# Five of nine sign passes read from PSUM, routing's small steps and four subtractions moved to GpSimd, and a new set of order offsets

## The chip, the cores and the metric

The kernel runs on one core of one Trainium2 chip. The metric is the time of one execution on the device in microseconds (us), lower is better. Times given for a kernel are medians of several runs; the profile is of one more execution, whose own time is given beside its span.

The core's engines are named as the profile names them: PE is the matrix engine (PEld its weight loads), DVE the vector engine, ACT the scalar engine, POOL is GpSimd, and SP is the engine that here only starts transfers. Matrix products land in PSUM, all else lives in SBUF.

## The reference, cut to what matters

Attention with a top-32 mask over 8 x 8 heads of 576 rows of 64 numbers, and then a mixture of 8 experts in which every token that is not skipped takes one expert:

```python
scores = scale * q @ k.T                                  # 64 heads, 576 x 576
kth = np.partition(scores, -32, axis=-1)[..., -32:-31]
scores = np.where(scores >= kth, scores, -1e9)
attn = exp(scores - max) / (sum + 1e-9)
x = (attn @ v) -> 4608 tokens x 512
do_compute = x @ w_skip > 0
logits = x @ w_gate;  e_idx = argmax(logits, axis=1)
gate_w = softmax(logits)[e_idx]
out = x;  out[do_compute] += gate_w * (relu(x @ w1[e_idx]) @ w2[e_idx])
```

Every row of scores needs its 32nd largest value, so each row of 576 scores is searched, not only exponentiated.

## The kernel before, in words

**Attention, some 860 us.** Two heads make a pair; there are 32 pairs (`NP`), and nine row tiles of 128 rows (`NR`) in each, 288 in all. For one row tile the function `row` records these steps:

- PE computes 128 x 576 scores into one of three PSUM buffers of rows (`qk`, L652). The class `Hold` keeps the buffer until its readers have given it back.
- DVE finds the eight largest of each of seven chunks (`chunk`, L662), and then the 24 largest of those 56 (`cand`: L668 and L670 by turns, five steps, each of which needs the one before).
- ACT copies the scores from PSUM to SBUF (`take`, L704). After it the PSUM buffer is free: `take` is its only reader beside the chunk search.
- ACT takes the sign of each score against the 24th largest (`above_out`, L684), with the sum of the signs as a second output. It reads the SBUF copy, and its bias is one number per partition (a column of the tile `cl`).
- POOL multiplies copy and signs (`push_out`, L707), DVE fills nine more columns (`fill`, L716) and takes the eight largest of what is left (`window`, L728); the last of these is the threshold.
- ACT writes the penalty (`below_out`, L725): again from the SBUF copy, with one number per partition as bias.

When a pair's rows are done, nine "units" compute the transposed scores in the same three PSUM buffers (L867, L869), subtract the penalties (L874) and are read by one exponential on ACT (L899). Products with V, sums, and the gate's logits follow.

**Routing.** After the batches 0 to 3, after 4 to 6 and after 7 (`GROUPS`), the function `route` turns the gate's logits into lists of tokens: a chain of some 20 small steps of at most 128 x 160 elements, all on DVE, with one exponential and one copy on ACT and one product on PE between them (L410 to L450), and then per batch the lists (`lists`, L469 to L487), partly on POOL. The first two groups run during attention, the third at its end.

**Experts, some 300 us.** Weights are split in a high part (ACT, `part_hi`, L1109) and a low part (DVE, `part_lo`, L1112), tokens are gathered by index (POOL, L1139), and PE does three products for one. The first expert's weights are split while the last pair is still at work.

**What sets the order.** Nothing is issued in the order in which it is written. Each step is put in a plan (`pl.add`) with its engine, a duration, a due time and the steps it needs; `Plan.run` then picks, engine by engine, the next step by readiness and due time and emits it. The due times are a row's number plus offsets from the table `K` and, for each of the nine rows of a pair, from `FINE`. The order that comes out is fixed in the program: on the chip each engine works its list from the top, and a step that is not ready holds up what stands behind it.

Of the kernel before, what the change touches and what calls it, by code (L numbers as in the profile page):

```python
# [36 lines left out]
OUT = (0, 1, 2, 3, 4, 5, 6, 7, 8)  # L37
PD = ()
TD = ()
PP = ()  # L40
SA = 1
AD = ()


@with_exitstack
def tile_kernel(ctx, tc, q, k, v, w_skip, w_gate, w1, w2, out):
# [1545 lines left out]
```

## Time and profile before

| | |
|---|---|
| time, median of 3 runs | 1180.88 us (1179.74 to 1182.52) |
| the profiled execution's own time / its span | 1182.15 / 1180.3 us |
| PE busy, share of the span | 1117.7 us, 95% |
| DVE | 1000.2 us, 85% |
| ACT | 931.8 us, 79% |
| POOL | 752.6 us, 64% |
| granted PE clock over the span | 0.98 of full speed |

The span is the time from the first to the last instruction. A record's duration can overlap the one before it on its engine by some tenths of a us, so a group's count times its mean is more than the time it took. PE's busy time is modelled and says little. The busy time of the engines has to be read by stage: in attention PE, DVE and ACT are all busy for nearly the whole time, in the experts' stage PE alone is.

### The profile page before, as it was taken

What the parts mean: (1) busy time and instruction counts of PE and PEld (TensorE: products, weight loads), DVE (VectorE), ACT (ScalarE), POOL (GpSimd) and SP (SyncE); (2) the same over time, 40 slices, a digit from 0 to 9 for tenths busy, and PEclk for the clock granted to TensorE, in tenths of its full rate; (3) what the DMA queues carried; (4) which work ended last, traced back from release to release, by engine and by line L of the source; (5) the groups of instructions that cost most, each with busy time, mean ns of one, the idle gap of its engine ahead of it and who ended that gap; (6) DMA issues with size and microseconds to landing.
All of it is one profiled execution on the core that took longest, in us unless ns stands there. A gap on an engine that the chain in (4) does not pass through costs nothing. (4 is left out here: it accounts for less than half of the span.)

```text
span 1180.3 us, 37612 instructions
## 1 busy us (share of the span) xinstructions
PE 1117.7 (95%) x13012; PEld 947.0 (80%) x13012; DVE 1000.2 (85%) x5250; ACT 931.8 (79%) x1965; POOL 752.6 (64%) x997
## 2 busy tenths in 40 slices
PE   4899999999999999999999999999889999999996
PEld 3778888888888888788877878877778988888885
DVE  8999999999999999999999999999954756655531
ACT  5999999999999999999998999999862533333320
POOL 7778888777888877788875999777772112222210
PEclk8799999999999999999998999999999999999998
DMA  5545555644556554455544454443065654454300
GB/s 122 123 113 122 134 129 131 159 115 113 124 135 145 139 134 113 115 129 137 141 121 120 105 131 124 123 115 83 22 191 181 197 164 149 152 162 156 116 19 25
DMA packets 197404, 148.42 MB, mean 126 GB/s; under 512 B 100898, under 2 KB 162850, under 8 KB 197204
## 3 DMA queue, kind: packets, MB, share of 16 engines
q1 hardware_dynamic: 190340, 135.54, 44.8%
q0 software_dynamic: 3840, 9.47, 2.5%
q8 instruction: 105, 1.72, 0.6%
q10 hardware_dynamic: 3024, 0.90, 0.3%
q14 instruction: 95, 0.78, 0.2%
HBM read 68.31 MB, written 25.31 MB: 79 GB/s over the span
## 5 line engine op out<-in xcount | busy, mean ns | idle before, releaser
L707 POOL TENSOR_TENSOR xw<-xc,r 128x576 f32<-128x576 f32 x288 | 370.3, 1286 | 148.8 <-ACT r L684 143.4
L662 DVE MAX8 cand<-r 128x8 f32<-128x82 f32 (+1 forms) x2016 | 366.7, 234 | 3.0 <-PE r L652 2.9
L684 ACT ACTIVATE r<-xc,cl 128x576 bf16<-128x576 f32 x288 | 224.8, 780 | 16.3 <-DVE cl L668 15.3
L725 ACT ACTIVATE PEN<-xc,wn 128x576 bf16<-128x576 f32 x288 | 224.5, 780 | 3.7 <-DVE wn L728 3.6
L728 DVE MAX8 wn<-xw 128x8 f32<-128x585 f32 x288 | 217.2, 754 | 2.4 <-POOL xw L707 2.2
L867 PE MATMUL r<-QH,KK 128*128 128x256 f32 (+1 forms) x640 | 190.3, 324 | 10.1 <-ACT PT L899 4.5
L704 ACT ACTIVATE xc<-r 128x576 f32<-128x576 f32 x288 | 188.6, 655 | 9.5 <-DVE cand L662 3.9
L652 PE MATMUL r<-KK,QH 128*128 128x288 f32 x640 | 162.2, 344 | 14.0 <-ACT xc L704 6.6
L869 PE MATMUL r<-QL,KK 66*128 66x256 f32 (+1 forms) x640 | 174.5, 300 | 0.0
L668 DVE MAX8 cl<-cand 128x8 f32<-128x28 f32 (+2 forms) x864 | 166.7, 193 | 4.4
L899 ACT ACTIVATE PT<-r 128x576 f32<-128x576 f32 x256 | 166.9, 654 | 3.1 <-PE r L874 2.9
L1146 POOL DMA_INDIRECT out_dram<-ot,idx x24 | 24.5, 1022 | 213.8 <-DVE ot L1145 167.2
L1112 DVE TENSOR_TENSOR lo<-raw,hi 128x1024 fp32r<-128x1024 f32 x64 | 79.2, 1241 | 72.0 <-ACT hi L1109 71.1
L652 PE MATMUL r<-KK,QL 66*128 66x288 f32 x640 | 135.1, 302 | 0.0
L867 PEld LDWEIGHTS r<-QH,KK 128*128 128x128 f32 x640 | 119.0, 192 | 17.5 <-ACT PT L899 7.4
L874 PE MATMUL r<-nbi,PEN 128*128 128x128 bf16 (+1 forms) x1632 | 132.8, 217 | 0.0
L652 PEld LDWEIGHTS r<-KK,QH 128*128 128x128 f32 x640 | 98.2, 196 | 41.0 <-ACT PT L899 12.2
L1109 ACT ACTIVATE hi<-raw 128x1024 fp32r<-128x1024 f32 x64 | 67.2, 1055 | 71.6 <-PE py L1241 71.4
L869 PEld LDWEIGHTS r<-QL,KK 66*128 66x128 f32 x640 | 119.9, 193 | 0.3 <-issue 0.2
L652 PEld LDWEIGHTS r<-KK,QL 66*128 66x128 f32 x640 | 103.9, 194 | 0.3 <-issue 0.3
L1221 ACT ACTIVATE hh<-ph 128x352 fp32r<-128x352 f32 (+2 forms) x72 | 31.1, 433 | 92.5 <-PE ph L1218 89.4
L670 DVE MATCH_REPLACE8 cand<-cl,cand 128x28 f32<-128x28 f32 x576 | 103.3, 179 | 0.0
(256 smaller groups left out, 2575.4 us busy)
## 6 DMA issues: line engine op xcount, KB each, us to landing
raw<-in_moe_w_dram SPq DMA_DIRECT2D x64, 512.0 KB
KK<-HI SPq DMA_DIRECT2D x62, 288.0 KB
QH<-HI SPq DMA_DIRECT2D x124, 144.0 KB
KK<-LO SPq DMA_DIRECT2D x62, 144.0 KB
QL<-LO SPq DMA_DIRECT2D x62, 144.0 KB
raw<-in_k_dram SPq DMA_DIRECT2D x64, 128.0 KB
V<-in_v_dram SPq DMA_DIRECT2D x32, 256.0 KB
raw<-in_q_dram SPq DMA_DIRECT2D x62, 128.0 KB
```

Source lines behind the costliest of these rows:

```text
L652: nc.tensor.matmul(R(u, w), t[0:k0, c:c + P], KH[i2][0:k0, HB * hd + u:HB * hd + w], start=(k0 == P and x == 0), stop=(k0 < P and x == len ...
L662: nc.vector.max(C[s][:, c], R(CH[c], CH[c + 1]))
L668: nc.vector.max(L[:, 4 * r:4 * r + 8], c)
L684: nc.scalar.activation(RR[s], XC[s], AF.Sign, bias=CL[p][:, i, 23:24], scale=-ODD, accum_out=CN[:, s:s + 1])
L704: nc.scalar.activation(XC[s], R(), AF.Copy)
L707: nc.gpsimd.tensor_tensor(xw()[:, 0:S], XC[s], RR[s], op=OP.mult)
L725: nc.scalar.activation(pen, XC[s], AF.Relu, bias=least, scale=-1.0)
L728: nc.vector.max(WN[p][:, i], XW[s] if out_ else R())
L867: nc.tensor.matmul(t, KH[i2][:, ks], QH[i2][:, qs], start=(y == 0), stop=False)
L869: nc.tensor.matmul(t, KO[i2][:, ks], QL[i2][0:D + 2, qs], start=False, stop=False)
L874: nc.tensor.matmul(rb[:, O + c:O + c + z - a], PEN[p][:, PS * i + REM + c0 - o:PS * i + REM + c0 - o + P], nbi[:, a:z], start=False, stop= ...
L899: return pl.add("ACT", 0.535, due + K["ex"] + FINE["ex"][at], lambda: nc.scalar.activation(dst, st["r"], AF.Exp, scale=scale), x, give=[h])
```

## The change

`SG` names five of the nine row tiles of a pair (0, 2, 4, 6, 8). For these the sign pass reads the scores from PSUM, not the SBUF copy; the PSUM buffer then has two readers, `take` and the sign pass, and is free after the later one. The planner's duration for such a sign pass is 0.629 instead of 0.765. `push_out` now waits for `take` by itself. In the routing of the first two groups the steps with `pool=` go to POOL (two fused steps are cut in two), in the third group all stay on DVE. The low parts of the first four weight pieces go to POOL. All numbers of `K` and `FINE` are new.

```diff
-LOOK, GAIN, KEEP = 0.164, 7.176, 67.94
+LOOK, GAIN, KEEP = 0.118, 8.156, 71.051
...
+SG = (0, 2, 4, 6, 8)
...
-        lock = 0.25
+        lock = 0.0 if end else 0.7
+        G_ = V_ if end else nc.gpsimd
...
-        def later(f, dur, *after):
-            x = pl.add("DVE", dur, st["due"], f, u, after)
+        def later(f, dur, *after, pool=None):
+            x = pl.add("DVE", dur, st["due"], f, u, after) if end or not pool else \
+                pl.add("POOL", 0.19 + 0.0022 * pool, st["due"], f, u, after)
...
-        later(lambda: V_.tensor_sub(T["d"], l8, bc(T["mx"])), wide + lock)
-        vx = later(lambda: V_.scalar_tensor_tensor(T["val"], T["d"], 0.0, wb, op0=OP.is_equal, op1=OP.mult), wide + lock)
+        later(lambda: G_.tensor_tensor(T["d"], l8, bc(T["mx"]), op=OP.subtract), wide, pool=n * E)
+        later(lambda: G_.tensor_scalar(T["val"], T["d"], 0.0, None, op0=OP.is_equal), wide, pool=n * E)
+        vx = later(lambda: G_.tensor_tensor(T["val"], T["val"], wb, op=OP.mult), wide, pool=n * E)
...
-        later(lambda: V_.scalar_tensor_tensor(mb, lb[:, :, E], 0.0, mb, op0=OP.is_gt, op1=OP.mult), small + lock)
+        later(lambda: G_.tensor_scalar(T["col"], lb[:, :, E], 0.0, None, op0=OP.is_gt), small, pool=n)
+        later(lambda: G_.tensor_tensor(mb, T["col"], mb, op=OP.mult), small, pool=n)
...
-        later(lambda: V_.tensor_scalar(T["gt"], T["gt"], 1e-9, None, op0=OP.add), small + lock)
+        later(lambda: G_.tensor_scalar(T["gt"], T["gt"], 1e-9, None, op0=OP.add), small, pool=n)
...
-        later(lambda: V_.tensor_add(T["val"], T["sr"][:, 0:n], base[:, b0:b0 + 1].to_broadcast([P, n, E])), wide + lock, srx)
-        later(lambda: V_.tensor_mul(T["val"], T["val"], T["oh"]), wide + lock)
+        later(lambda: G_.tensor_tensor(T["val"], T["sr"][:, 0:n], base[:, b0:b0 + 1].to_broadcast([P, n, E]), op=OP.add), wide, srx, pool=n * E)
+        later(lambda: G_.tensor_tensor(T["val"], T["val"], T["oh"], op=OP.mult), wide, pool=n * E)
...
-        later(lambda: V_.tensor_copy(lo, T["ri"]), small)
-        later(lambda: V_.tensor_sub(hi, T["rk"], lo), small + lock)
+        later(lambda: G_.tensor_copy(lo, T["ri"]), small, pool=n)
+        later(lambda: G_.tensor_tensor(hi, T["rk"], lo, op=OP.subtract), small, pool=n)
...
-        h = Hold(RW, 1 if out_ else 2)
+        h = Hold(RW, 1 if out_ and i not in SG else 2)
...
-            nc.scalar.activation(RR[s], XC[s], AF.Sign, bias=CL[p][:, i, 23:24], scale=-ODD, accum_out=CN[:, s:s + 1])
+            nc.scalar.activation(RR[s], R() if i in SG else XC[s], AF.Sign, bias=CL[p][:, i, 23:24], scale=-ODD, accum_out=CN[:, s:s + 1])
...
-            rr = A("ACT", 0.765, s + D_["kt"] + J("kt"), above_out, x, tx, PENNED.get(s - 3), lag=-0.06)
+            rr = A("ACT", 0.629 if i in SG else 0.765, s + D_["kt"] + J("kt"), above_out, x, None if i in SG else tx, PUSHD.get(s - 3), give=[h] if i in SG else (), lag=-0.06)
...
-        PARTED.append(pl.add("DVE", 1.13, D0 + 1 + i, lambda i=i: part_lo(0, i), x))
+        PARTED.append(pl.add("POOL", 2.4, D0 + 1 + i, lambda i=i: part_lo(0, i, nc.gpsimd), x))
```

Four more steps of one number per row (L446, L449 and L450 of before among them) move in the same way.

Three places in the order of the program show what moved. The first is DVE in the routing of batches 0 to 3; `rval` is the tile of ranks, `cand`, `cl`, `wn` and `xw` belong to row tiles. Before:

```order
L668 MAX cl<-cand 128x8
L437 TENSOR_TENSOR rval<-rsr,base 128x160
L670 MATCH_REPLACE cand<-cl,cand 128x7x4
L438 TENSOR_TENSOR rval<-rval,roh 128x160
L668 MAX cl<-cand 128x8
L716 TENSOR_SCALAR xw<-wo,CN 128x9
L670 MATCH_REPLACE cand<-cl,cand 128x7x6
L439 TENSOR_REDUCE rmx<-rval 128x20
```

The same two steps now, on POOL, among the products of row tiles (`xw`):

```order
L443 TENSOR_TENSOR rval<-rsr,base 128x160
L714 TENSOR_TENSOR xw<-xc,r 128x576
L444 TENSOR_TENSOR rval<-rval,roh 128x160
L714 TENSOR_TENSOR xw<-xc,r 128x576
L752 COPY FL<-cl 128x9
L753 COPY FL<-wn 128x9
```

The two additions and products of ranks have left DVE's list; the sum over them (L439, now L445) stays there and waits for POOL.

The second place is DVE in the middle of attention, two row tiles; `r_146` to `r_148` are the three PSUM buffers. Before:

```order
L668 MAX cl<-cand 128x8
L728 MAX wn<-xw 128x8
L670 MATCH_REPLACE cand<-cl,cand 128x7x4
L716 TENSOR_SCALAR xw<-wo,CN 128x9
L668 MAX cl<-cand 128x8
L662 MAX cand<-r_146 128x8
L670 MATCH_REPLACE cand<-cl,cand 128x7x6
L662 MAX cand<-r_146 128x8
L668 MAX cl<-cand 128x8
L662 MAX cand<-r_146 128x8 x5
```

And now, at the same distance from the start:

```order
L675 MAX cl<-cand 128x8
L669 MAX cand<-r_147 128x8
L677 MATCH_REPLACE cand<-cl,cand 128x7x4
L669 MAX cand<-r_147 128x8
L675 MAX cl<-cand 128x8
L669 MAX cand<-r_147 128x8
L677 MATCH_REPLACE cand<-cl,cand 128x7x6
L669 MAX cand<-r_147 128x8
L675 MAX cl<-cand 128x8
L669 MAX cand<-r_147 128x8 x3
```

One chunk of the next row tile now stands between any two of the five steps of a row tile.

The third place is the end of attention; `sum` belongs to the last pair, `lo_...` are the low parts of the first expert's weights. Before, on DVE, among the last products with V:

```order
L1007 TENSOR_TENSOR xb<-pt,sm 128x2x2x64
L1012 TENSOR_TENSOR lgt<-pt,sm 128x36
L1112 TENSOR_TENSOR lo_17802<-raw_17794,hi_17798 128x1024
L1112 TENSOR_TENSOR lo_17803<-raw_17795,hi_17799 128x1024
L1112 TENSOR_TENSOR lo_17804<-raw_17796,hi_17800 128x1024
L1112 TENSOR_TENSOR lo_17805<-raw_17797,hi_17801 128x1024
```

And now, on POOL, around the gathers of the first expert's tokens (DMA):

```order
L933 TENSOR_TENSOR sum<-PT_125 128x576
L1199 MEMSET xg_17824 128x1560
L1028 TENSOR_TENSOR lg<-lg,lgt 128x2x2x9
L1028 TENSOR_TENSOR lg<-lg,lgt 64x9 x2
L1145 DMA xg_17824<-xd,idx_202 128x520 x2
L1118 TENSOR_TENSOR lo_17820<-raw_17812,hi_17816 128x1024
L933 TENSOR_TENSOR sum<-PT_123 128x576
L1118 TENSOR_TENSOR lo_17821<-raw_17813,hi_17817 128x1024
L1118 TENSOR_TENSOR lo_17822<-raw_17814,hi_17818 128x1024
L1118 TENSOR_TENSOR lo_17823<-raw_17815,hi_17819 128x1024
```

The four low parts have gone from DVE to POOL, and the last pair's second sum stands behind the first of them.

## Rows read from the trace of the kernel before

**Rows 1.** Busy us of each engine by stretch (instructions), clock, DMA.
```profile
200.00:350.00 150.00, 149.02 (x2054) 124.84 (x2047) 147.98 (x896) 148.62 (x329) 118.68 (x154) 1.00 0.54 130
...
600.00:660.00 60.00, 55.17 (x724) 46.31 (x722) 58.28 (x317) 51.68 (x113) 43.28 (x57) 0.91 0.46 111
780.00:840.00 60.00, 56.06 (x778) 44.73 (x771) 58.97 (x341) 53.72 (x119) 39.73 (x55) 1.00 0.34 83
860.00:900.00 40.00, 34.92 (x515) 29.98 (x508) 23.66 (x72) 18.92 (x38) 20.55 (x41) 0.96 0.74 228
```
**Rows 2.** Groups of DVE, 60 to 820 us: count, busy, mean, idle before.
```profile
L662 DVE MAX8 cand<-r 128x8 f32<-128x83 f32 x521 | 122.1, 235 | 0.9 <-PE r L652 0.9
```
**Rows 3.** Groups of DVE by line, 60 to 845 us: routing steps that move.
```profile
L442 DVE CAST rank<-rri 128x20 f32<-128x20 int32 (+1 forms) x2 | 2.6, 1276 | 0.0
L446 DVE TENSOR_SCALAR rcol<-m 128x20 f32<-128x20 f32 (+1 forms) x2 | 2.1, 1038 | 0.0
L437 DVE TENSOR_TENSOR rval<-rsr,base 128x160 f32<-128x160 f32 (+1 forms) x2 | 1.9, 954 | 0.0
L450 DVE TENSOR_TENSOR base<-base,rsr 128x8 f32<-128x8 f32 x2 | 1.9, 938 | 0.0
L449 DVE TENSOR_SCALAR rcol<-rcol 128x20 f32<-128x20 f32 (+1 forms) x2 | 1.7, 872 | 0.0
L415 DVE SCALAR_TENSOR_TENSOR m<-lg,m 128x20 f32<-128x20 f32 (+1 forms) x2 | 1.7, 864 | 0.0
L438 DVE TENSOR_TENSOR rval<-rval,roh 128x160 f32<-128x160 f32 (+1 forms) x2 | 1.5, 748 | 0.0
...
L433 DVE TENSOR_SCALAR rgt<-rgt 128x20 f32<-128x20 f32 (+1 forms) x2 | 0.7, 370 | 0.0
```
**Rows 4.** Groups of ACT, 60 to 820 us.
```profile
L725 ACT ACTIVATE PEN<-xc,wn 128x576 bf16<-128x576 f32 x262 | 204.5, 781 | 3.1 <-DVE wn L728 3.1
L684 ACT ACTIVATE r<-xc,cl 128x576 bf16<-128x576 f32 x260 | 203.2, 781 | 10.7 <-DVE cl L668 9.8 <-DVE lgt L1012 0.5
L704 ACT ACTIVATE xc<-r 128x576 f32<-128x576 f32 x261 | 171.3, 656 | 8.0 <-DVE cand L662 2.6
```
**Rows 5.** Groups of ACT, 0 to 60 us.
```profile
L613 ACT ACTIVATE QH<-TT 64x576 fp32r<-64x576 f32 x4 | 2.7, 681 | 0.1
```
**Rows 6.** Timeline from 485 us: start, us, engine, step; one row tile's buffer, a unit's.
```profile
485.31 0.80 PE L652 MATMUL r<-KK,QH 128*128 128x288 f32 x4
...
487.39 0.24 DVE L662 MAX8 cand<-r 128x8 f32<-128x83 f32 x1
...
489.78 0.64 ACT L704 ACTIVATE xc<-r 128x576 f32<-128x576 f32 x1
...
491.36 0.38 PE L867 MATMUL r<-QH,KK 128*128 128x320 f32 x1
491.46 0.78 ACT L684 ACTIVATE r<-xc,cl 128x576 bf16<-128x576 f32 x1
...
492.90 0.62 ACT L899 ACTIVATE PT<-r 128x576 f32<-128x576 f32 x1
```
**Rows 7.** Timeline from 490 us, DVE: a step with another ahead of it.
```profile
490.63 0.23 DVE L662 MAX8 cand<-r 128x8 f32<-128x82 f32 x1
...
490.84 0.18 DVE L670 MATCH_REPLACE8 cand<-cl,cand 128x42 f32<-128x42 f32 x1
```
**Rows 8.** Timeline from 857 us, DVE: a step right behind what it reads.
```profile
857.09 0.20 DVE L668 MAX8 cl<-cand 128x8 f32<-128x42 f32 x1
...
857.41 0.19 DVE L670 MATCH_REPLACE8 cand<-cl,cand 128x42 f32<-128x42 f32 x1
```
**Rows 9.** Groups of POOL, 60 to 870 us.
```profile
L707 POOL TENSOR_TENSOR xw<-xc,r 128x576 f32<-128x576 f32 x274 | 352.4, 1286 | 145.2 <-ACT r L684 139.9 <-DMA QH<-HI 2.0 <-DVE wn L728 0.2
L565 POOL TENSOR_TENSOR LO<-TT,HI 128x640 fp32r<-128x640 f32 x58 | 90.7, 1563 | 0.0
```
**Rows 10.** Timeline from 871 us: the start of the first expert.
```profile
873.22 1.51 POOL L927 TENSOR_TENSOR sum<-PT 128x576 f32<-128x576 f32 x1
...
884.26 0.37 PE L1216 MATMUL ph<-xh,hi 128*128 128x224 f32 x1 [3.11 <-ACT xh L1156]
```

More of the change, by code (lines that the diff above doesn't have):

```diff
@@ L30 @@
         ("PE", "PE"): 0.0}
-LOOK, GAIN, KEEP = 0.164, 7.176, 67.94
-DRAIN, TURN = 0.2, 39.21
-K = dict(qk=-6.436, cand=-7.822, kt=-6.355, push=-12.756, count=2.92, window=2.675, kth=4.11, rf=40.955, pen=-24.387, u0=6.301, u1=10.019, av=-0.812, a0=2.517, a1=7.268, a2=2.062, co=45.04, sm=-27.744, ca=48.91, tx=-2.41, rt=9.211, rd=-4.985, rs=1.779, pp=12.011, ps=0.546, mx=16.505, f3=5.424, f4=2.403, f5=-9.516, ex=-28.018, us=-0.294, cs=-44.193, ch=0.074, ce=-10.653, lg=3.943, ld=11.234, hl=6.901, hs=-0.757, moe=22.067)
@@ L441, in route @@
         later(lambda: V_.tensor_single_scalar(T["ri"], T["ri"], P - 1, op=OP.bitwise_and), small + lock)
-        later(lambda: V_.tensor_copy(lo, T["ri"]), small)
-        later(lambda: V_.tensor_sub(hi, T["rk"], lo), small + lock)
+        later(lambda: G_.tensor_copy(lo, T["ri"]), small, pool=n)
+        later(lambda: G_.tensor_tensor(hi, T["rk"], lo, op=OP.subtract), small, pool=n)
         later(lambda: V_.scalar_tensor_tensor(T["ok"], hi, float(NB * P), mb, op0=OP.is_lt, op1=OP.mult), small + lock)
-        later(lambda: V_.tensor_scalar(T["col"], mb, -float(NB), float(EB + 1), op0=OP.mult, op1=OP.add), small)
+        later(lambda: G_.tensor_scalar(T["col"], mb, -float(NB), float(EB + 1), op0=OP.mult, op1=OP.add), small, pool=n)
         later(lambda: V_.scalar_tensor_tensor(T["col"], hi, 1.0 / P, T["col"], op0=OP.mult, op1=OP.add), small + lock)
         later(lambda: V_.scalar_tensor_tensor(T["col"], T["ok"], 0.0, T["col"], op0=OP.is_gt, op1=OP.mult), small + lock)
-        rx = later(lambda: V_.tensor_scalar(T["col"], T["col"], 1.0, None, op0=OP.subtract), small)
-        bx = pl.add("DVE", 0.07, st["due"], lambda: V_.tensor_add(base[:, b0 + nb], base[:, b0], T["sr"][:, n]), rx)
+        rx = later(lambda: G_.tensor_scalar(T["col"], T["col"], 1.0, None, op0=OP.subtract), small, pool=n)
+        bx = later(lambda: G_.tensor_tensor(base[:, b0 + nb], base[:, b0], T["sr"][:, n], op=OP.add), small, pool=E)
         if b0 + nb == B - 1:
@@ L635, in row @@
         i2 = p % NQ
+        PEN[p] = PEN_[p % 2]
         out_ = i in OUT
-        h = Hold(RW, 1 if out_ else 2)
+        h = Hold(RW, 1 if out_ and i not in SG else 2)
         R = lambda u=0, w=S: h.t[:, LO_ + u:LO_ + w]
@@ L766, in row @@
             tx = A("DVE" if i in TD else "ACT", 0.67 if i in TD else 0.537, s + D_["tx"] + J("tx"), take, chs, OUTB[-3:-2], give=[h], lag=0.01)
-            rr = A("ACT", 0.765, s + D_["kt"] + J("kt"), above_out, x, tx, PENNED.get(s - 3), lag=-0.06)
+            rr = A("ACT", 0.629 if i in SG else 0.765, s + D_["kt"] + J("kt"), above_out, x, None if i in SG else tx, PUSHD.get(s - 3), give=[h] if i in SG else (), lag=-0.06)
             fx = A("DVE", 0.129, s + D_["push"] + J("fill"), fill, rr, OUTW[-2:-1])
-            x = [A("POOL", 1.31, s + D_["push"] + J("push"), push_out, rr, OUTW[-2:-1]), fx]
+            PUSHD[s] = A("POOL", 1.31, s + D_["push"] + J("push"), push_out, rr, tx, OUTW[-2:-1])
+            x = [PUSHD[s], fx]
         else:
@@ L786, in row @@
         if out_:
-            kx = PENNED[s] = A("POOL" if i in PP else "ACT", 1.56 if i in PP else 0.672, s + D_["rf"] + J("rf"), below_out, x, PENNED.get(s - 1), TU.get(p - 2) if i == 0 else None)
+            kx = PENNED[s] = A("POOL" if i in PP else "ACT", 1.56 if i in PP else 0.672, s + D_["rf"] + J("rf"), below_out, x, TU.get(p - 2))
             OUTB.append(kx)
@@ L793, in row @@
             FLAGGED[p] = A("POOL", 0.47, s + 3, flags, kx, WINS[p])
-    RF, XC, XW, OUTB, OUTW, WINS = {}, {}, {}, [], [], {}
+    RF, XC, XW, OUTB, OUTW, WINS, PUSHD = {}, {}, {}, [], [], {}, {}
     PS = S + REM
@@ L1109, in part_hi, with part_lo @@
         nc.scalar.activation(WHI[w][i], WRAW[w][i], AF.Copy)
-    def part_lo(w, i):
-        nc.vector.tensor_sub(WLO[w][i], WRAW[w][i], WHI[w][i])
+    def part_lo(w, i, eng=nc.vector):
+        eng.tensor_tensor(WLO[w][i], WRAW[w][i], WHI[w][i], op=OP.subtract)
     def part(w, i):
```

6 lines of the change are left out of this document (3 added, 3 removed).

## The prediction

> **What bounds the kernel now.** I read the table of stages first, then the groups of instructions by shape for DVE, ACT and POOL in attention, then the timeline of a few row tiles. The chain that ended last is of no use here: it holds four pieces after 1164 us, far from the change.
>
> In the even middle of attention DVE is busy for 147.98 of 150 us, ACT for 148.62, PE for 149.02 [rows 1]. Three engines look full, but they are not full in the same way. PE's ends are modelled. ACT's and DVE's records are real, so I ask where a full engine gives way when its load rises. That is seen where routing adds steps to DVE: from 600 to 660 us and from 780 to 840 us DVE stays at 58.28 and 58.97 of 60 us while ACT falls to 51.68 and 53.72 and PE to 55.17 and 56.06 [rows 1]. So DVE sets the pace and the other two wait for it. DVE also hardly ever waits for PE: its idle time ahead of the first and the last chunk of a row tile is 0.9 us over 521 such instructions [rows 2]. A saving on DVE in attention therefore counts nearly in full, and a saving on ACT or POOL counts only through what it lets DVE do.
>
> **The change part by part.**
>
> Routing's steps. Eight lines that move have 2.6 + 2.1 + 1.9 + 1.9 + 1.7 + 1.7 + 1.5 + 0.7 = 14.1 us on DVE in the first two groups, 16 instructions [rows 3]. These are long for 15 to 160 elements because they stand still behind POOL: the addition of base and counts over eight numbers means 938 ns. A record overlaps its forerunner by some 0.08 us: the chunk at 490.63 ends at 490.86 and the replacement that started at 490.84 ends 0.16 later, at 491.02, though it lasted 0.18 [rows 7], and the whole group of chunk searches is shorter than count times mean in the same way; with 16 x 0.08 = 1.3 off, 12.8 us go. Three more lines that move are under 0.7 us each and I leave them out. What is added back: each group now has seven places at which a DVE step waits for a POOL step that may stand behind one product of 1286 ns [rows 9]. Fourteen places cost between nothing, when other rows' work fills the list between, and 14 x 1.29 = 18 us. The order leaves row work between them, so I take 2 us, near the lower end. POOL's own load grows by some 30 short steps on an engine that idles 145.2 us ahead of its products [rows 9], so it costs nothing itself. Term: -12.8 + 2 = -10.8.
>
> The order on DVE. A replacement right behind the search whose result it reads ends 0.31 us after it (857.29 to 857.60) [rows 8]; with another row's chunk between, it adds 0.16 (490.86 to 491.02) [rows 7]. The difference is 0.15 us. I counted in both orders how often one of the five steps stands directly behind the step it reads: 264 times before, 219 now. That is 45 x 0.15 = 6.8 us less. The product with the reciprocal of a row's sum stands directly behind that reciprocal 25 times now and 2 times before; at the same price 23 x 0.15 = 3.5 more. Term: -3.3, with -6.8 and 0 as ends.
>
> The sign pass from PSUM. The sign costs 781 ns from SBUF, the copy from PSUM 656 [rows 4], so the most that the other source can give is 125 ns. But the two differ in more than the source: the sign has a bias of one number per partition, the copy has none. The copy of the first heads reads SBUF, has no such bias and takes 681 ns for the same 576 columns [rows 5]. So the source is worth 681 - 656 = 25 ns and the rest goes with the bias, which stays; the penalty pass, which has such a bias and no sum, takes the same 781 [rows 4]. I take 25 ns, since that row differs from the copy in nothing but the source and the number of partitions: 160 x 0.025 = 4 us of ACT, against 20 us at the other end. ACT is not the bound, so on the path I put 0.
> The Trainium skill has a rule on this, in "ScalarE: Activation LUTs", section "What ACT_TABLE_LOAD costs": a bias given as a per-partition pointer costs some 93 ns more than an immediate one. By the rule 93 of the 125 ns are the bias and 32 the source, 160 x 0.032 = 5 us of ACT (an estimate from that page); the trace agrees with it, at 100 and 25.
> The planner was told 0.629 instead of 0.765, that is 0.136 less. If the chip gives 0.025, ACT runs behind its list by 5 x 0.111 = 0.56 us in each pair. The upper end of its cost is 32 x 0.56 = 18 us, if nothing absorbs it; ACT idles 10.7, 8.0 and 3.1 us ahead of its three large groups [rows 4], and what it owes in all is not more than before, so I put it at 0 too.
>
> The PSUM buffers. This is what the change takes away. A row tile's buffer is written from 485.31 and free at 490.42, when the copy ends: 5.1 us. With the sign as second reader it would be free at 492.24, 1.8 us later; a unit's buffer lives from 491.36 to 493.52, 2.2 us [rows 6]. A pair lasts 26.2 us (nine copies; 261 in 760 us, [rows 4]), so the three buffers have 78.6 us, of which 9 x 5.1 + 9 x 2.2 = 65.7 are held and 12.9 free. Five signs a pair take 5 x 1.8 = 9 of these. What is left is 3.9 us for 18 uses, 0.22 us each, instead of 0.72. PE then loads just in time and no longer ahead. Today DVE loses 0.9 us to that in all [rows 2]; no row shows it with so little room. At one end it costs nothing, because the 5.1 us hold time in which the buffer only waits for DVE; at the other it is the rival below. I take +4 us, some four times what DVE loses now.
>
> The low parts. On POOL 640 columns take 1563 ns [rows 9], so 1024 take some 2.5 us and four take 10. DVE is not the bound there (23.66 of 40 us, [rows 1]), so nothing is gained by freeing it. On POOL the first of them stands ahead of the last pair's second sum, which started at 873.22 [rows 10] and may start up to 2.5 us later. PE then waited 3.11 us for the gathered tokens before the first expert [rows 10]; that covers it. Were the cover gone, 2.5 us would be added. Term: 0.
>
> Sum: -10.8 - 3.3 + 0 + 4 + 0 = -10.1 us. Against the profiled execution's own time of 1182.15 us (span 1180.3) that is 1172.0; the median of the runs lies 1.3 us below that execution, so I predict 1171 us.
>
> **The rivals.**
>
> 1. The PSUM buffers become the bound (slower). Price: if a change of use needs 0.37 us on the mean, half of today's 0.72, the shortage is 18 x (0.37 - 0.22) / 3 = 0.9 us in a pair, 29 us in 32 pairs; less the 14 gained, 15 us slower, 1196. It decides from the point at which the shortage eats the 14 us, 0.44 us a pair, that is from 0.29 us a use. For it: ACT and DVE are full, so the second reader is often late. Against it: the buffer's 5.1 us hold 2.1 us between the first matmul and the first chunk [rows 6], which can shrink.
>
> 2. The gain comes out elsewhere (same). PE, at 55 to 56 of 60 us where routing runs [rows 1], takes over as the bound as soon as DVE is freed, and the waits for POOL cost 9 instead of 2 us. Then -10.1 + 7 and a little more, 1179. For it: three engines within 2% of each other in the even stretch. Against it: PE's ends are modelled, and DVE keeps its own pace in every stretch.
>
> 3. The sign does give 125 ns (faster). Then ACT is freed of 20 us, the products on POOL that wait 139.9 us for the sign [rows 9] start earlier, and the order fits the planner's prices. DVE's own idle time, some 2 us in 150 [rows 1], 11 in attention, mostly goes and the buffers are freed earlier: -10.1 - 6 - 3, 1162. For it: only that no row shows such an instruction. Against it: [rows 5].
>
> 4. Routing's chain is late at the end of attention. The gathers need the second group's lists. Seven visits to POOL, each behind a product of 1.29 us [rows 9], lengthen that chain by up to 9 us; the lists are due when attention ends, so some 5 of them may be seen: 1176. For it: the lists' last steps on POOL stand few places ahead of the gathers. Against it: in the new order they stand ahead of both of the last pair's sums.
>
> **How the numbers follow.** Forecast 0.45, its own range 1163 to 1177; rival 1 0.22; rival 2 0.14; rival 3 0.10; rival 4 0.09. A difference under 0.2% (2.4 us) can't be told from none here. Faster takes 0.43 of the forecast, 0.09 of rival 3, 0.08 of rival 4, 0.04 of rival 2 and 0.03 of a mild rival 1: 0.67. Same takes 0.09 of rival 2, 0.02 of the forecast and 0.01 each of rivals 3 and 4: 0.13. Slower is 0.19 of rival 1 and 0.01 of rival 2: 0.20. The range's low end is the sum with every favourable bound (12.8 + 6.8 + 4 us of ACT seen by DVE, 24 us: 1157); the high end is half way into rival 1, 1188.
>
> **What would show it.** DVE's time in routing: the moved lines gone from DVE, ACT and PE nearer to full from 600 to 660 us. The sign from PSUM as a group of its own: near 756 ns means that the source is worth 25, near 656 that it is worth 125. The buffers: idle time of PE ahead of L652's successor, and of DVE ahead of the first chunk, over 0.9 us in attention, is what rival 1 needs; tens of us there and a longer pair in the even stretch prove it. The low parts: some 2.5 us each on POOL, and PE's wait ahead of the first expert shorter or the same. The forecast is wrong if the even stretch, in which nothing but the sign and the order changed, goes slower than 26.2 us a pair by more than 0.3.

## The result, and the profile after

The changed kernel takes 1195.14 us (median of 4 runs, 1193.92 to 1195.46), the kernel before 1180.93: 1.0118 times as long, 95% interval 1.01 to 1.0135. It is slower by 14 us where 10 us faster was forecast. The profiled execution took 1195.45 us, span 1193.5.

The same stretches after the change, busy time of each engine as in [rows 1]:

```profile
200.00:350.00 150.00, 146.16 (x2057) 120.62 (x2055) 144.09 (x877) 145.87 (x322) 116.39 (x148) 1.00 0.53 125
600.00:660.00 60.00, 58.34 (x808) 48.86 (x796) 57.06 (x349) 57.16 (x126) 50.94 (x72) 1.00 0.54 126
780.00:840.00 60.00, 54.93 (x761) 44.05 (x754) 57.77 (x343) 53.94 (x116) 43.15 (x66) 0.99 0.34 78
860.00:900.00 40.00, 33.79 (x516) 26.90 (x516) 21.48 (x61) 20.19 (x41) 28.57 (x46) 0.91 0.43 141
```

In the even stretch from 200 to 350 us all engines do less in the same time: PE, DVE and ACT each lost 2.7 to 3.9 us of 150. No engine became fuller, so none became the limit by its own load. From 600 to 660 us, where routing ran before, ACT rose from 51.68 to 57.16 and PE from 55.17 to 58.34, as forecast. The granted clock of PE in that stretch rose too, from 0.91 to 1.00 of full speed: before, it fell from 2.4 to 1.2 GHz for some 10 of the 60 us (an estimate from the 0.91), the first time after PE had been busy for only 3.27 us from 610 to 615. No run separates what that was worth.

How long a pair takes is read from the last of its nine thresholds (`window`). The rows of pairs 6 and 15 in the timeline of DVE, in the kernel before:

```profile
197.45 0.75 DVE L728 MAX8 wn<-xw 128x8 f32<-128x585 f32 x1
...
428.05 0.75 DVE L728 MAX8 wn<-xw 128x8 f32<-128x585 f32 x1
```

and the same two after:

```profile
202.18 0.75 DVE L733 MAX8 wn<-xw 128x8 f32<-128x585 f32 x1
...
438.57 0.75 DVE L733 MAX8 wn<-xw 128x8 f32<-128x585 f32 x1
```

Nine pairs lie between: 230.60 / 9 = 25.62 us a pair before, 236.39 / 9 = 26.27 after. "The even stretch" means these nine pairs below. Busy time of each engine over them (as in [rows 1]: PE, PEld, DVE, ACT, POOL), before and after:

```profile
197.45:428.05 230.60, 229.13 (x3206) 192.15 (x3205) 227.51 (x1378) 228.42 (x505) 183.64 (x235) 1.00 0.54 130
202.18:438.57 236.39, 230.71 (x3216) 190.18 (x3208) 226.38 (x1379) 230.19 (x505) 185.09 (x234) 1.00 0.54 126
```

DVE works 1.1 us less in the nine pairs, and stands idle for 10.0 us instead of 3.1: the longer pair is DVE waiting. The list of DVE's waits over the nine pairs has no entry before. After, its longest (us, times, longest) is the fill of nine columns behind the sign, and the rest of the list, waits for PE, is 0.7 us:

```profile
DVE xw L723 <- ACT r L691: 5.3, 18, 0.3
```

The chain that ended last, which the profile of the changed kernel has through attention, agrees. In one pair, from 349.90 to 376.17 us, it lies on DVE for 18.9 us, on ACT for 4.8, on POOL for 1.3. Pieces of it (start, us, what):

```profile
351.08 0.55 ACT xc L711
351.63 0.72 ACT r L691 x2
352.35 1.08 ACT PT L905 x2
353.43 0.76 ACT r L691 x2
...
365.10 0.84 ACT r L691 x2
...
366.07 1.30 POOL xw L714
```

For the kernel before, the profile has no chain there to compare. The rows of the thresholds, followed through the program, give the account of the whole:

| where | after against before, us |
|---|---|
| last threshold of pair 22 (start and even stretch) | +14.2 |
| pair 23, with the first routing group | -5.2 |
| pairs 24 to 31, with the second | -2.2 |
| from the last threshold to the first expert's first product | +5.7 (28.3 instead of 22.6) |
| from there to the end | +0.6 |

The sum, +13.1, is the difference of the spans, 13.2. Routing did give a gain; the even stretch and the end of attention took away more than twice as much.

Where the waits went is seen in the groups by shape from 60 to 820 us (idle time ahead, and who ended it). Before, the fill of nine columns on DVE and the first products of row tiles and units on PE:

```profile
L716 DVE TENSOR_SCALAR xw<-wo,CN 128x9 f32<-128x9 f32 x260 | 55.3, 213 | 2.5 <-ACT r L684 2.1
L652 PE MATMUL r<-KK,QH 128*128 128x288 f32 x578 | 143.8, 339 | 7.4 <-ACT xc L704 4.2 <-ACT PT L899 0.7
L867 PE MATMUL r<-QH,KK 128*128 128x256 f32 x288 | 81.4, 299 | 4.1 <-ACT PT L899 3.6 <-ACT xc L704 0.4
```

After, the same with the first chunk [rows 2], the sign in its two forms and the copy [rows 4], the product on POOL [rows 9], and two of the moved routing steps:

```profile
L669 DVE MAX8 cand<-r 128x8 f32<-128x83 f32 x515 | 116.7, 237 | 2.9 <-PE r L659 2.4
L723 DVE TENSOR_SCALAR xw<-wo,CN 128x9 f32<-128x9 f32 x258 | 54.8, 213 | 15.7 <-ACT r L691 14.3
L659 PE MATMUL r<-KK,QH 128*128 128x288 f32 x574 | 141.2, 335 | 2.5 <-ACT PT L905 1.2 <-ACT r L691 1.0
L873 PE MATMUL r<-QH,KK 128*128 128x256 f32 x287 | 85.5, 314 | 14.6 <-ACT r L691 11.2 <-ACT xc L711 0.9 <-ACT PT L905 0.6
L711 ACT ACTIVATE xc<-r 128x576 f32<-128x576 f32 x258 | 168.3, 653 | 8.3 <-DVE cand L669 6.9 <-DVE xw L723 0.6 <-POOL LO L571 0.3
L691 ACT ACTIVATE r<-r,cl 128x576 bf16<-128x576 f32 x144 | 107.1, 743 | 7.1 <-DVE cl L675 6.6
L691 ACT ACTIVATE r<-xc,cl 128x576 bf16<-128x576 f32 x114 | 89.3, 783 | 4.2 <-DVE cl L675 2.4 <-DVE sm L1004 0.2 <-DVE lgt L1018 0.2
L714 POOL TENSOR_TENSOR xw<-xc,r 128x576 f32<-128x576 f32 x274 | 352.6, 1288 | 114.6 <-ACT r L691 107.3 <-DVE cl L675 3.1 <-ACT xc L711 2.0
L443 POOL TENSOR_TENSOR rval<-rsr,base 128x160 f32<-128x160 f32 (+1 forms) x2 | 1.0, 480 | 0.0
L456 POOL TENSOR_TENSOR base<-base,rsr 128x8 f32<-128x8 f32 x2 | 0.5, 229 | 0.0
```

The sign from PSUM takes 743 ns, from the copy 783: the source is worth 40 ns. The fill stands 14.3 us behind signs that the plan believed 0.11 us shorter, and a unit's first product stands 11.2 us behind a sign that still holds its PSUM buffer. These are the two waits that one would blame, and in this order the first is most of DVE's new idle time. The experiments show that taking either away doesn't give the old pair back.

The end of attention after the change, from the timeline:

```profile
876.13 0.63 SPq L368 DMA_DIRECT2D xd<-xb  x1
877.24 0.18 DVE L1137 TENSOR_TENSOR idx<-ti,LS 128x24 int32<-128x24 f32 x1
879.71 1.30 POOL L1145 DMA_INDIRECT xg<-xd,idx  x1 [3.41 <-DMA xd<-xb]
881.31 1.01 POOL L1145 DMA_INDIRECT xg<-xd,idx  x1 [0.31 <-DMA out_dram<-xb]
882.35 2.36 POOL L1118 TENSOR_TENSOR lo<-raw,hi 128x1024 fp32r<-128x1024 f32 x1
883.20 7.52 DVE L1028 TENSOR_TENSOR lg<-lg,lgt 128x36 f32<-128x36 f32 x1
888.51 1.09 PE L1158 MATMUL pa<-identF,xg 128*128 128x128 f32 x4 [4.34 <-DMA xg<-xd,idx]
896.80 0.35 PE L1222 MATMUL ph<-xh,hi 128*128 128x224 f32 x1
```

POOL stands 3.41 us ahead of the first gather. The index is ready at 877.42; the last 2.3 us are spent until a store of tokens issued at 876.13 has landed. PE's list has the transposes of both gathered tiles ahead of the last products with V, so PE stands 4.34 us for the second gather and has those products still to do: the first expert begins at 896.80, not 884.26 [rows 10].

### The profile page after: what moved, and what is told of

Its sections match the earlier page's. It is cut to its first block, busy times and chain, and to the rows that moved or that the text cites. A ratio compares the mean times of both kernels' runs of the same rounds, so it can differ in the third digit from the quotient of the medians.

```text
span 1193.5 us, 37517 instructions
## 1 busy us (share of the span) xinstructions
PE 1120.2 (94%) x13012; PEld 939.5 (79%) x13012; DVE 990.3 (83%) x5226; ACT 935.7 (78%) x1965; POOL 767.6 (64%) x1027
## 4 chain that ended last, share of the span: by engine, by line
DVE 44%; PE 28%; ACT 16%; issue 4%; POOL 3%; DMA 3%; SPq 1%; ACTq 0%; POOLq 0%; DVEq 0%
DVE cand L669 18%; DVE wn L733 9%; ACT r L691 6%; DVE cand L677 5%; DVE cl L675 5%; PE py L1245 4%; PE py L1247 4%; PE py L1246 4%; ACT PT L905 3%; ACT xc L711 3%; PE ph L1222 3%; PE ph L1223 3%; PE ph L1224 3%; DVE xw L723 2%; POOL xw L714 2%
## 5 line engine op out<-in xcount | busy, mean ns | idle before, releaser
L669 DVE MAX8 cand<-r 128x8 f32<-128x82 f32 (+1 forms) x2016 | 386.6, 234 | 4.7 <-PE r L659 3.8
L873 PE MATMUL r<-QH,KK 128*128 128x256 f32 (+1 forms) x640 | 192.6, 328 | 21.3 <-ACT r L691 14.3
L711 ACT ACTIVATE xc<-r 128x576 f32<-128x576 f32 x288 | 187.3, 653 | 11.5 <-DVE cand L669 9.0
L905 ACT ACTIVATE PT<-r 128x576 f32<-128x576 f32 x256 | 163.7, 655 | 4.9 <-PE r L880 4.7
L675 DVE MAX8 cl<-cand 128x8 f32<-128x56 f32 (+2 forms) x864 | 160.2, 191 | 3.5
L1118 DVE TENSOR_TENSOR lo<-raw,hi 128x1024 fp32r<-128x1024 f32 x60 | 73.5, 1224 | 71.4 <-ACT hi L1115 69.8
L691 ACT ACTIVATE r<-r,cl 128x576 bf16<-128x576 f32 x160 | 118.9, 743 | 9.7 <-DVE cl L675 9.2
L691 ACT ACTIVATE r<-xc,cl 128x576 bf16<-128x576 f32 x128 | 100.1, 782 | 5.7 <-DVE cl L675 3.8
L677 DVE MATCH_REPLACE8 cand<-cl,cand 128x28 f32<-128x28 f32 (+1 forms) x576 | 102.4, 179 | 0.0
```

Source lines behind the costliest of these rows:

```text
L669: nc.vector.max(C[s][:, c], R(CH[c], CH[c + 1]))
L675: nc.vector.max(L[:, 4 * r:4 * r + 8], c)
L677: nc.vector.match_replace(c, L[:, 4 * r - 4:4 * r + 4], c, LOWEST)
L691: nc.scalar.activation(RR[s], R() if i in SG else XC[s], AF.Sign, bias=CL[p][:, i, 23:24], scale=-ODD, accum_out=CN[:, s:s + 1])
L711: nc.scalar.activation(XC[s], R(), AF.Copy)
L873: nc.tensor.matmul(t, KH[i2][:, ks], QH[i2][:, qs], start=(y == 0), stop=False)
```

## The experiments

All ratios are to the kernel before on the same chip, with their 95% intervals; 17 kernels were run. "Numbers" means `LOOK`, `GAIN`, `KEEP`, `K` and `FINE`; "hold" means that the plan gives the PSUM buffer back after the sign and not after the copy; "edited waits" are edits of the plan that the change also makes and that I had passed over: a sign waits for the product three rows earlier instead of the penalty, and a penalty no longer for the one before it.

### The change's parts

**The order kept, the copy read.** The plan of the changed kernel word for word, but on the chip a sign reads the copy wherever the copy stands ahead of it, in 285 of 288 row tiles.

```diff
-... R() if i in SG else XC[s], AF.Sign, ...
+... XC[s] if s in XC else R(), AF.Sign, ...
```

> The changed kernel with its order of instructions kept word for word; only the five sign passes read the SBUF copy again (where the copy stands ahead of them), so that a PSUM buffer is free after the copy. Measured in the changed kernel: an undisturbed pair takes 26.3 us instead of 25.6, and a sign from PSUM 743 ns instead of 783. Theory BUFFER (the second reader of the PSUM buffers slows the pair): the pair falls to 25.6 to 25.8 and the whole to about 1178 to 1182. Rival ORDER (the new order itself is slower, whoever reads what): the pair stays at 26.3, or 26.5 with 5 x 0.04 us more of ACT, the whole at 1195 to 1200.

1202.28 us, 1.018 (1.0163 to 1.0196). Two of its groups, and DVE's wait for the sign in nine pairs:

```profile
L723 DVE TENSOR_SCALAR xw<-wo,CN 128x9 f32<-128x9 f32 x256 | 54.6, 213 | 25.8 <-ACT r L691 23.4
L873 PE MATMUL r<-QH,KK 128*128 128x256 f32 x285 | 82.9, 307 | 1.5 <-ACT PT L905 1.2
...
DVE xw L723 <- ACT r L691: 9.3, 19, 0.5
```

The wait of PE for the buffer is gone, 14.6 to 1.5 us, and the kernel is 7 us slower still: 26.57 us a pair, 0.30 more, of which 5 x 40 ns for the longer signs are 0.2. On the chip the second reader costs nothing that the shorter sign doesn't give back. The loss sits in the order of the instructions.

**Routing on POOL alone.** The kernel before with the change's `route` and nothing else.

> The kernel before with routing's small steps on POOL and nothing else: old offsets, signs from the copy, low parts on DVE. Theory ROUTING (DVE's 12.8 us in the first two groups come back nearly in full, as the changed kernel's pairs 22 to 31 show): 1166 to 1172. Rival LATE LISTS (the chain of the second group with seven visits to POOL is late for the gathers): the rows of attention end 10 us earlier, the first expert only 3 to 5, 1176.

1184.91 us, 1.0033 (1.002 to 1.0045), above both forecasts. The even stretch stays at 25.6. At pair 23 the rows are 6.2 us earlier, by pair 27 only 0.8, at the last threshold 5.6; then all of it is lost again. Its timeline at the end of attention:

```profile
865.88 5.23 DVE L1117 TENSOR_TENSOR lo<-raw,hi 128x1024 fp32r<-128x1024 f32 x4 [1.24 <-ACT hi L1114]
866.38 5.69 POOL L483 TENSOR_SCALAR rlo<-i,rank 128x128 bf16<-128x128 f32 x3
872.37 0.23 DVE L492 TENSOR_TENSOR LS<-LS,pt 128x72 f32<-128x72 f32 x1 [0.27 <-PE pt L489]
873.62 0.18 DVE L1136 TENSOR_TENSOR idx<-ti,LS 128x24 int32<-128x24 f32 x1
```

Four low parts stand ahead of the lists' last addition, and beside them three comparisons on POOL take 5.69 us, which take 0.6 each elsewhere.

**The low parts back on DVE**, in the changed kernel:

```diff
-pl.add("POOL", 2.4, D0 + 1 + i, lambda i=i: part_lo(0, i, nc.gpsimd), x)
+pl.add("DVE", 1.13, D0 + 1 + i, lambda i=i: part_lo(0, i), x)
```

> The changed kernel with the four low parts on DVE as before. In the changed kernel one addition of 36 columns on DVE takes 7.5 us while POOL does the low parts, and the first expert starts 9.5 us later against the end of the rows than before. Theory GATHER (the gathers are late, for their indices and for a store ahead of them, and PE's list has them ahead of the last pair's products): the long addition goes, the first expert starts at most 2 us earlier, 1193 to 1195. Rival PORT (the addition that POOL holds up is what delays the tail): 6 to 8 us earlier, 1187 to 1189.

1195.54 us, 1.0124 (1.0108 to 1.0141), the same as the changed kernel and far from the 1187 to 1189 of PORT. The addition of 7.52 us falls to 0.57 (the row of `lg` at 883.95 there) and nothing ends earlier: it was not on the path.

**The signs alone**, with the hold, the edited waits and the price 0.629, in the kernel before with its old numbers:

```diff
-h = Hold(RW, 1 if out_ else 2)
+h = Hold(RW, 1 if out_ and i not in SG else 2)
...
-... XC[s], AF.Sign, ...
+... R() if i in SG else XC[s], AF.Sign, ...
...
-A("ACT", 0.765, ..., above_out, x, tx, PENNED.get(s - 3), ...)
+A("ACT", 0.629 if i in SG else 0.765, ..., above_out, x, None if i in SG else tx, PUSHD.get(s - 3), give=[h] if i in SG else (), ...)
```

> The kernel before with the five sign passes from PSUM and their planner's duration of 0.629 and nothing else: old offsets, planned anew; routing and low parts on DVE. Theory BUFFER: pairs of 26.2 us or more, 1195 to 1205. Rival ORDER (only the new offsets cost): pairs near 25.6, 1176 to 1184.

1211.31 us, 1.0255 (1.0238 to 1.0272), 26.59 us a pair: slower than either theory had it.

**The new numbers without the signs** (the changed kernel with `SG = ()`).

> The changed kernel with no row tile in SG: new numbers, routing and low parts on POOL, but all signs from the copy, at the planner's 0.765, the PSUM buffer given back after the copy. Keeping the changed kernel's order and reading the copy gave 26.5 us a pair, so the slow pair lies in the order. Theory PLANNED HOLD (the planner, told that five buffers a pair are held to the sign, can't feed the engines): with the hold gone the pair falls to 25.6 to 25.8, the whole to 1178 to 1184, with the changed kernel's tail. Theory PRICE (the planner's 0.629 for a pass that takes 0.72): also 25.6 to 25.8. Theory NUMBERS (the new offsets make worse pairs by themselves): 26.1 or more, 1190 to 1200.

1197.13 us, 1.0137 (1.0115 to 1.016); its pairs are uneven, 24.9 to 28.3 us in the even stretch. So neither half of the change is good by itself, and together they are no better than the numbers alone.

### The plan

**The true price.** The changed kernel with 0.726, near what the chip takes, in place of 0.629.

> The changed kernel with one planner's number changed: 0.726 instead of 0.629 for a sign from PSUM, which is what the changed kernel's profile shows between the starts of such a pass and the next instruction. Theory PRICE: the pair falls from 26.3 to 25.6 to 25.8, the whole to 1180 to 1185. Theory PLANNED HOLD: the pair stays at 26.1 to 26.5, 1192 to 1200.

1194.39 us, 1.0105 (1.0088 to 1.0122), 26.05 us a pair. The two waits, and DVE's longest waits in nine pairs:

```profile
L723 DVE TENSOR_SCALAR xw<-wo,CN 128x9 f32<-128x9 f32 x257 | 54.1, 210 | 9.0 <-ACT r L691 7.1
L873 PE MATMUL r<-QH,KK 128*128 128x256 f32 x287 | 87.0, 319 | 3.8 <-ACT r L691 1.0 <-ACT PT L905 0.9
...
DVE sm L1004 <- PE pt L999: 4.7, 9, 0.6
DVE xw L723 <- ACT r L691: 0.4, 2, 0.3
```

Both are cut, 14.3 to 7.1 and 11.2 to 1.0 us, and a pair gains only 0.2 us: where DVE waited 5.3 us for the sign it now waits 0.4, and 4.7 for PE. The one price made another order with other waits. That the whole time is the same within 1 us is chance: the end of attention is 6.9 us shorter than in the changed kernel, pairs 24 to 31 are 6.9 us longer, and the experts 3.3.

**The hold in the plan alone.** The kernel before with hold and edited waits, old price, and the copy read.

```diff
-h = Hold(RW, 1 if out_ else 2)
+h = Hold(RW, 1 if out_ and i not in SG else 2)
...
-A("ACT", 0.765, ..., above_out, x, tx, PENNED.get(s - 3), ...)
+A("ACT", 0.765, ..., above_out, x, tx, PUSHD.get(s - 3), give=[h] if i in SG else (), ...)
```

> The kernel before with one thing changed in the plan: in the five row tiles the planner gives the PSUM buffer back only after the sign, as if the sign read it. The sign reads the copy and has its old duration of 0.765, so on the chip the buffer is free after the copy. Theory PLANNED HOLD: the order alone costs 0.5 to 1 us a pair, 26.2 to 26.6, the whole 1192 to 1212. Theory PRICE: 25.6 to 25.7, 1180 to 1184.

1210.47 us, 1.0242 (1.0213 to 1.0271), 26.5 us a pair: nothing is slower on the chip, only the plan believes in a longer hold. This looked like proof that the planned hold is the cause.

**Signs from PSUM at the true price**, old numbers (as the signs alone, 0.726).

> The kernel before with the five signs from PSUM and the true duration of 0.726 in the plan (with 0.629 it had 26.6 us a pair and 1211). Theory PRICE: 25.6 to 25.8 a pair, 1178 to 1184. Theory PLANNED HOLD: 26.2 to 26.7, 1195 to 1212; at most 0.2 us a pair below the copy read in the same plan.

1217.36 us, 1.0313 (1.0293 to 1.0332), 27.0 us a pair, above both forecasts: a truer price makes this plan worse.

**Two controls.** The kernel before with one number changed: the price of five signs to 0.726, or `LOOK` to 0.118. Nothing else differs.

> Control. The kernel before with one thing changed in the plan: five of nine sign passes priced at 0.726 instead of 0.765; they read the copy, and the buffer is given back after the copy, as before. Nothing that is computed changes, only the order. Theory PLANNED HOLD (the longer hold in the plan costs a pair 0.7 to 1 us): a change of price alone leaves a pair of the even stretch at 25.6 to 25.8 us, 1178 to 1188. Rival FIT (the order before is one that its numbers were fitted to, and any new plan is worse): 26.2 to 26.6 us a pair, 1198 to 1212, as the runs with the planned hold were.

> Second control. The kernel before with one number of the planner changed to its new value: LOOK 0.118 instead of 0.164 (how long the planner lets an engine wait for a more urgent step). Nothing that is computed changes. Theory PLANNED HOLD: 25.6 to 25.8 us a pair, 1178 to 1188. Rival FIT: 26.2 to 26.6 us a pair, 1198 to 1212.

1198.84 us, 1.016 (1.0142 to 1.0177), and 1183.49, 1.0016 (1.0005 to 1.0027). The price alone, with no hold and no work changed, costs as much as the whole change: 25.9 us a pair in the even stretch, 5 us in the first five pairs, and an end of attention 3.4 us longer. The theory of the planned hold as the one cause fell here. Its rival FIT, any new plan is far worse, did no better: it had 1198 to 1212 us for `LOOK` too, and that control costs 2 us (25.79 us a pair, 3.2 us less at the end of attention). How far a number moves the time is not told by its kind.

**The new numbers without hold**, at both prices (the changed kernel, copy read, buffer given back after the copy).

> The changed kernel, but all sign passes read the copy, and the plan gives the buffer back after the copy; the price of 0.629 for five of nine signs stays, so the numbers of the planner and its prices are all those of the changed kernel. Theory PLANNED HOLD (the longer hold is what makes the pair longer): 25.6 to 25.8 us a pair, 1176 to 1186. Rival FIT (the new numbers were fitted with the hold, and any plan off its fit is worse): 26.1 us a pair or more, uneven, 1192 to 1205.

> As the run of the new numbers without hold, with 0.726 instead of 0.629 as the price. Theory PLANNED HOLD: 25.6 to 25.8 us a pair, 1176 to 1186, as the numbers then meet a plan with more room. Rival FIT: 26.0 us a pair or more, 1190 to 1205, and one price moves it by 3 us or more either way.

1205.99 us, 1.02 (1.0182 to 1.0219), and 1190.64, 1.0077 (1.006 to 1.0093). PLANNED HOLD is wrong in both; at the change's own price, taking the hold away makes it 11 us slower.

**The edited waits alone**, at both prices, old numbers.

> The kernel before with only the change's edits of the plan's waits: a sign pass waits in the plan for the product three rows earlier instead of the penalty three rows earlier, a penalty no longer for the one before it. The sign passes read the copy at the old price, the buffer is given back after the copy. Theory HOLD+FIT (the hold has a cost of its own): 25.6 to 26.0 us a pair, 1180 to 1199, well under the 1210.5 that the run with these edits and the hold had. Rival WAITS (the edits of the waits already throw the order off as far): 1205 to 1213.

> As the run with the edits of the waits alone, with 0.726 as the price of five of nine signs. Theory HOLD+FIT: 1190 to 1205, 10 us or more under the 1217.4 of the run with the hold at this price. Rival WAITS: 1210 to 1220.

1195.87 us, 1.0117 (1.0083 to 1.0151), and 1192.5, 1.0089 (1.006 to 1.0117). Together (us a run, `-` not run; on different chips, on which the kernel before takes 1180.9 to 1182.1):

| | price 0.765 | 0.726 | 0.629 |
|---|---|---|---|
| old numbers | 1180.9 | 1198.8 | - |
| and edited waits | 1195.9 | 1192.5 | - |
| and hold | 1210.5 | 1217.4 (PSUM read) | 1211.3 (PSUM read) |
| new numbers, edited waits (routing and low parts as changed) | 1197.1 | 1190.6 | 1206.0 |
| and hold (PSUM read) | - | 1194.4 | 1195.1, the change |

With the old numbers the hold costs 14.6 us at the old price, and 24.9 at 0.726; with the new ones 3.8 and -10.9. Only the first of the four is the hold alone, as in the others the signs read PSUM too. The price of 0.726 in place of 0.765 is worth +18, -3, +7 (with the PSUM read) or -7 us, by what stands beside it. No part shows a cost of its own that holds beside the others: each makes another order, and every other order of the table is worse than the first.

### The end of attention

**Low parts behind the index**, in the kernel before with routing on POOL:

```diff
-PARTED.append(pl.add("DVE", 1.13, D0 + 1 + i, lambda i=i: part_lo(0, i), x))
+PARTED.append(pl.add("DVE", 1.13, D0 + 1 + i, lambda i=i: part_lo(0, i), HIGH[i], x))   # x: here the index
```

> The kernel before with routing of the first two groups on POOL (the earlier run with that alone: 1184.9), and the first four low parts, still on DVE, made to stand behind the index computation. In the earlier run the row tiles ended 5.6 us earlier, and then four low parts on DVE (865.88 to 871.11) stood ahead of the last addition to the lists (872.37), while three comparisons on POOL beside them took 5.69 instead of 1.8 us. Theory LATE LISTS: take the low parts out of that place and the index comes 2 to 5 us earlier, the first expert too: 1180 to 1183. In the new order the last addition still stands behind a reciprocal that waits for a sum of PE, so the low end is not reached. Rival (the first expert waits for PE's own list, not for the index): no change, 1185.

1182.83 us, 1.0019 (1.001 to 1.0029), within the expected range, but not for its reason: the index came at 876.2, later than 873.6, as the plan also moved in pairs 27 to 31 (rows end 2.9 us later). Inconclusive by itself.

**The lists of batches 6 and 7 on DVE**, which waits there, on top of it:

```diff
+late = lambda j: ("DVE", 0.2, V_) if end or (b0 + nb == B - 1 and j == nb - 1) else None
...
-e, dur, eng = on(True)
+e, dur, eng = late(j) or on(True)
...
-e, dur, eng = on(t > 1)
+e, dur, eng = late(j) or on(t > 1)
```

> As the run with the low parts behind the index, and the steps of the lists of batches 6 and 7 (products and comparisons) all on DVE, which waits there. Theory LATE LISTS: the chain of lists ends about when the last row tile's thresholds do, the index near 866 instead of 873.6, the first expert some 5 us earlier than in the run with routing on POOL alone: 1176 to 1179, faster than the kernel before (1181). Rival (PE's own list, the last pair's products with V, holds the first expert): 1181 to 1185.

1178.79 us, 0.999 (0.9977 to 1.0003). The index comes at 867.1, 6.5 us earlier than with routing alone, the first expert 3.1 us earlier (880.9). Half is lost on ACT:

```profile
877.54 0.60 ACT L1162 ACTIVATE xh<-pa 128x512 fp32r<-128x512 f32 x1 [5.20 <-PE pa L1158]
877.57 0.62 ACTq L366 DMA_DIRECT2D xd<-xb  x1
...
879.56 0.66 ACTq L367 DMA_DIRECT2D out_dram<-xb  x1
880.27 0.60 ACT L1162 ACTIVATE xh<-pt 128x512 fp32r<-128x512 f32 x1 [2.12 <-issue]
```

Four stores, issued by ACT itself at 0.65 us each, stand between the two copies of the gathered tokens. They stand there before the change too.

**Those stores behind both copies.**

```diff
+put = lambda *after: store(b, ..., due, DONE[p] + list(after), p == NP - 1)
...
+XBFREE[NP - 1] = LASTPUT[0](*XT)   # the last pair's put, after the tokens' copies
```

> As the run with the lists on DVE (1178.8), and the last pair's four stores, which ACT issues between the two copies of the gathered tokens (877.57 to 880.2 there; the second copy stood 2.1 us behind them), planned behind both copies. Theory LATE LISTS in its wider form (the first expert waits for the gathered tokens alone): the second copy comes 2.1 us earlier, the first expert too: 1176 to 1178, faster than the kernel before. Rival (PE's first product waits for split weights anyway, or the stores come back in a later wait): 1178 to 1181.

1176.57 us, 0.9953 (0.9939 to 0.9966): faster than both kernels. The same place now:

```profile
877.62 0.60 ACT L1166 ACTIVATE xh<-pa 128x512 fp32r<-128x512 f32 x1 [5.10 <-PE pa L1162]
878.42 0.60 ACT L1166 ACTIVATE xh<-pt 128x512 fp32r<-128x512 f32 x1 [0.20 <-PE pt L1162]
```

The first expert begins at 879.1. From the last threshold to there it is 22.3 us (22.6 before), and the last threshold comes 4.9 us earlier than before. The gain of routing on POOL is thus real, and is seen once the chain behind it is no longer than it was. No run has these edits of the end without routing on POOL.

## Why the prediction was wrong

The step that failed is the first: "DVE sets the pace and the other two wait for it", from which every saving on DVE was counted in full and ACT's part was put at 0 twice, for the shorter sign and for the planner's price. In the changed order DVE waits: its work in the even stretch fell by 1.1 us, as the sum wanted, and its idle time rose by 6.9, of which 5.3 lie behind signs on ACT. At 0.77 us a pair that is some 25 us in 32 pairs (an estimate), where the sum had nothing. That the engines were full in [rows 1] held for that one order, and it did not follow that one of them was at its limit: in the changed order PE, DVE and ACT are idle for 2.6 to 3.9% of the same stretch. Of the two stretches with routing from which the step was read, the one from 600 to 660 us had a lower clock of PE besides (0.91).

What makes DVE wait is the order as a whole. With the order kept and the second reader taken away the kernel is slower still; with one price changed and no work it is as slow. The sum priced instructions, and had no term for the order but "-3.3" for neighbours on DVE. By the eleven other plans in the table the kernel is 9 to 36 us slower than by the first; the largest term of the sum was 10.8. That the old numbers were fitted to the old plan is my reading. `LOOK` alone, which costs 2 us, shows that not every new plan is far worse.

- **Routing, -10.8.** The moved steps are short on POOL (229 ns for the addition over eight numbers instead of 938). But the rows gained 5.2 us in the first group and 2.2 after it in the changed kernel, 6.2 and in all 5.6 alone: half to two thirds. The 2 us for waits behind POOL were too few for the second group, which lost 5.7 us in pairs 26 and 27 of the run with routing alone and gave 4.8 back after them. There, from 718 to 749 us, POOL was busy for 29.86 us of 31 and DVE for 25.96, so POOL's load did cost something. (The overlap of 0.08 us that the term takes off is not in the rows that it names, which show 0.02; 194.47 + 0.75 against 195.14, a threshold and the next step on DVE, show it.)
- **The order on DVE, -3.3.** DVE's work in nine pairs is 227.51 us before and 226.38 after, some 4 us less in 32 pairs. The term is right, and idle time took more than it gave.
- **The sign's source, 25 ns.** 40 ns. Rival 3 (125 ns) is refuted. The new row also prices what is left: sign and copy, both from PSUM, take 743 and 653 ns, 90 apart; they differ in the bias, and in function and output type too. The Trainium skill ("ScalarE: Activation LUTs", section "What ACT_TABLE_LOAD costs") gives some 93 ns for a bias by per-partition pointer, and the 90 agree with it.
- **The planner's price, 0.** It did give the wait that was named, 14.3 us ahead of the fill. At the true price half of it went, nearly all in the even stretch, and a pair gained 0.2 of the 0.64 us, as other waits came. As a change of the plan a price moved the time by up to 18 us.
- **The PSUM buffers, +4.** PE's wait ahead of row tiles and units rose from 11.5 to 17.1 us, DVE's ahead of the first chunk from 0.9 to 2.9: 2 us for the 4, and far from the tens that rival 1 needed. Rival 1 had named 1196; that its number came out is luck, as the run with the order kept shows: without that wait of PE it is slower.
- **Low parts, 0.** Right: 2.36 us each and no effect.
- **The end of attention.** Rival 4 had 5 us for late lists and gave it 0.09; 5.7 came, by the gathers' wait for a store and the transposes' place in PE's list. In the run with routing alone it was the lists themselves. But the 5.7 come with the order as well: with the same routing and low parts, and no hold, the three plans of new numbers take 18.0 to 18.9 us from the last threshold to the first expert, where the kernel before takes 22.6.
- **The test that I had set** spoke of 26.2 us a pair as the even stretch. That was the mean from 60 to 820 us, with routing in it; the even stretch was 25.62. By its letter, 26.5, the changed kernel with its 26.27 passes it; by the right base it is slower by 0.64, twice the 0.3 allowed.

What stays open is which neighbourhoods make the first order so good, and whether numbers fitted anew to the true price and the hold would pass it. No run here searched for such numbers.

## What to carry to other kernels

When a planner writes the order, an edit of a price, a wait or a buffer's hold is a new program: make a control that changes one such number and no work, and see how far that moves the time, before any part is given a cost. Equally full engines in one stretch don't say which of them is the bound: look in the changed kernel at which of them now waits, and for whom. When an early part gets faster, follow the gain to the end of its stage: here it was lost behind four low parts, lists on POOL and four stores, and came back when these were moved.

## What the runs showed of the hardware

- One addition of 128 x 36 on DVE took 7.52 us (883.20 to 890.72; 0.19 in the run with routing alone) beside three subtractions and one sum on POOL, back to back until 890.66, and three comparisons on POOL took 5.69 us beside four subtractions on DVE. The Trainium skill ("SBUF — State Buffer", section "Who interferes with whom") says that an instruction of DVE with two inputs in SBUF contends with one of GpSimd that reads SBUF, as its second input comes through a read interface that they share. The rows agree, in both directions.
- Cutting the longest visible waits (14.3 to 7.1 and 11.2 to 1.0 us at the true price) moved the whole time by under 1 us and a pair by 0.2. Other waits came: that of the first chunk, 2.9 us in the changed kernel, is 8.2 in that run.
- A store issued by ACT itself took ACT's queue for 0.62 to 0.66 us; four of them ahead of a copy kept it for 2.12 us.
